# A gated mix of linear attention and a GLU in one kernel: the key sums with the values as stationary operand, 64-partition matmuls filled to 128, and another order of the stages

## The chip, the cores and the metric

One core of a Trainium2 chip runs the whole program. The time is device microseconds of one execution. Six streams of work matter in the profile: PE (matrix multiplication) and PEld (the loading of its stationary operand), DVE, ACT and POOL (elementwise engines), and SP, which here only issues DMAs. ACT and POOL issue DMAs too. Every engine works through its own list strictly in order, so one instruction that waits holds up all that stand behind it on that engine.

## The reference

The inputs are x (2048 tokens by 576), the attention weights, three GLU weights and a gate vector. Linear attention with 32 heads of 18 and a tanh-GELU GLU of width 4608 are mixed per token.

```python
def _A_ref(x, wqkv, wo):
    B, S, D = x.shape
    H = 32; Dh = D // H
    qkv = (x @ wqkv).reshape(B, S, 3, H, Dh).transpose(2, 0, 3, 1, 4)
    q, k, v = qkv[0], qkv[1], qkv[2]
    phi = lambda t: jnp.where(t > 0, t + 1, jnp.exp(t)) + 1e-6
    pq, pk = phi(q), phi(k)
    kv = jnp.einsum("bhsd,bhse->bhde", pk, v)
    z = jnp.einsum("bhsd->bhd", pk)
    num = jnp.einsum("bhqd,bhde->bhqe", pq, kv)
    den = jnp.einsum("bhqd,bhd->bhq", pq, z)[..., None] + 1e-6
    return (num / den).transpose(0, 2, 1, 3).reshape(B, S, D) @ wo

def _B_ref(x, w_gate, w_up, w_down):
    return (gelu(x @ w_gate) * (x @ w_up)) @ w_down

g = sigmoid((x * gate_w).sum(-1, keepdims=True))
return g * _A_ref(x) + (1 - g) * _B_ref(x)
```

## The kernel before

**Numbers.** Operands are split into a high part (written in fp32r) and a low part (the rest); a product is high x high + high x low + low x high.

**Key loop** (lines 187 to 238, up to 147 us). For each of 16 tiles of 128 tokens the kernel projects keys, values and the gate (42 matmuls), applies phi to the keys, and `kv_state` adds the tile's keys times values into `acc_a` and `acc_b`: for each of five groups of seven heads (the last has four), one matmul with the high keys and one with the low keys as stationary operand (126 columns, 72 in the last group), and the values as moving operand: two columns of ones, the high and the low values, 254 columns in all (146 in the last group). All four products come out, low by low too; the column of ones gives z.

**Stage order** (lines 440 to 735). The stages behind it are written out by hand as words in four lists; `run` calls them one after the other, and this sets the order of every engine. A word is a letter and one or two indices:

- `Qbg`, `abg`: the query projection of token block b (four blocks of 512 tokens) and column group g into one of three PSUM banks (14 matmuls of 512 columns, 10 for g = 4), and phi on ACT and DVE. `hbg` splits it on ACT and DVE; `dbg` adds it to the denominators (two matmuls, one for g = 4).
- `s`, `z`, `t`, `u`: copy out the state, write z to DRAM and read it back, mask and transpose the state on PE, split it. `n` makes the denominator's weights of z. `wg`, `ig`, `og`, `fg`: load wo's part, split it, multiply the state by it, store the result in DRAM; `lg`, `cg`: load that back and split it into KW.
- `rb`: the reciprocals of block b's denominators, in two halves. ACT copies one part of a half out of PSUM, DVE adds the other and inverts; SP stores 18 copies per head in DRAM (`rden_d`) and loads them back spread over the partitions (`rb`).
- `pbt`, `mbt`, `ebt`: scale the queries of token tile t (DVE, ACT, DVE), multiply by KW (28 matmuls of 288 columns into one of two pairs of banks; the last two use 64 partitions, since the last group has 64 rows), copy out on ACT with the gate and store by ACT's queue.
- `Xk`, `yk`, `Yk`: load a part of x, form four sums of token blocks on DVE, write their high parts on ACT and low parts on POOL into `xo`. The sums overwrite slots of `xo` that held blocks 2 and 3; `x` stores those in DRAM first (three DMAs). X1 and X2 are issued by POOL, into one buffer. `Wm`: load the first weights of the GLU. `Gk`, `gk`: the GLU's first products.

**The GLU** (from about 306 us) is a loop over 36 steps whose order is a table that stays as it is.

Of the kernel before, what the change touches and what calls it, by code (L numbers as in the profile page):

```python
# [21 lines left out]
NG = 5  # L22
# [5 lines left out]
CW = 126 + NG * 64 + 128  # L28
# [22 lines left out]
def tile_gated_mix(ctx, tc, xt, xs, wkv, wq, wo, wgu, wgt, wdn, cst, out):  # L51
# [8 lines left out]
    rden_d = {(b, h): dram.tile([H, DH, BS // 2], F32, name=f"rden_d{b}{h}") for b in range(NB) for h in range(2)}  # L60
# [130 lines left out]
    for v in vbuf:  # L191
        nc.vector.memset(f32(v).rearrange("p (g c) -> p g c", g=NG)[:, :, 0:2], 1.0)

    def kv_post(t, c, ps, part):
        if c == 0:
            pk[t] = (kp.tile([128, D], F32, name="e"), kp.tile([128, D], F32R, name="pkh"),
                     kp.tile([128, D], F32R, name="pkl"))
            vt[t] = vbuf[t % 2]
        r, ph, pl = pk[t]
        v3 = vt[t].rearrange("p (g c) -> p g c", g=NG)  # L200

        def k_part(lo, n):
# [24 lines left out]
    def kv_state(t):  # L227
        _, ph, pl = pk.pop(t)
        v = vt.pop(t)
        for g in range(NG):  # L230
            w = 2 + 2 * GR[g]
            mv = v[:, g * VW:g * VW + w]
            if g < 4:
                o = acc_a[:GR[g], g // 2, (g % 2) * VW:(g % 2) * VW + w]
            else:
                o = acc_b[:GR[g], 0, :w]
            for i, p in enumerate((ph, pl)):
                nc.tensor.matmul(o, p[:, GO[g]:GO[g] + GR[g]], mv,  # L238
                                 start=(t == 0 and i == 0 and g in (0, 2, 4)),
                                 stop=(t == NST - 1 and i == 1), skip_group_check=True)  # L240
# [160 lines left out]
    rs = [rp.tile([128, NG, BS], F32, name=f"r{i}") for i in range(3)]  # L401
    r_of = {2: rs[0], 3: rs[1], 0: rs[2], 1: rs[0]}
# [63 lines left out]
    wide = acc_a[:126, :, :2 * VW].rearrange("p a (b c) -> p a b c", b=2)  # L466
    last = acc_b[:72, 0]

    def sums_out():
        nc.vector.tensor_copy(zc[:126, :4].rearrange("p (a b) -> p a b", a=2), wide[:, :, :, 0])  # L470
        nc.vector.tensor_copy(zc[:72, 4:5], last[:, 0:1])

# [3 lines left out]
        nc.sync.dma_start(at(0, [[1, 126], [126, 4]]), zc[:126, :4])  # L476
        nc.sync.dma_start(at(504, [[1, 72], [1, 1]]), zc[:72, 4:5])
# [15 lines left out]

    turned = []

    def states_turn():
        tps = pair()
        turned[:] = [tps[:GR[g], g // 4, (g % 4) * 126:(g % 4) * 126 + GR[g]] for g in range(NG)]
        for g in range(NG):
            R = GR[g]  # L500
            nc.tensor.transpose(turned[g], kvm[:R, g, :R], ident[:R, :R])
# [27 lines left out]
    def head_out(g):  # L529
# [3 lines left out]
        kh, kl = kvt[:R, g, 0, :R], kvt[:R, g, 1, :R]  # L533
# [557 lines left out]
```

## Time and profile before

| | us |
|---|---|
| median of 3 runs (lowest, highest) | 1527.63 (1524.12, 1532.23) |
| the profiled execution | 1529.19 |
| its span, first to last instruction | 1527.4 |
| PE busy in the span | 1505.2 |
| key loop with its start, from the span's start to the first query | 146.8 |
| stage order, first query to the last token tile's output | 159.6 |

A row that groups instructions reads: line, engine, operation, output<-inputs, shapes, count, then busy time, mean ns of one, idle time before them and what ended it. A row of the chain of waits has a start, a length and what the time went to. PE's matmuls overlap, so the mean of one is longer than the distance of two starts; distances are taken from the chain.

### The profile page before, as it was taken

To read this page: it belongs to the slowest core of one execution; us is meant where nothing else is said; L and a number is where in the kernel's file an instruction comes from. 1 tells how busy PE (TensorE), PEld (TensorE's weight loads), DVE (VectorE), ACT (ScalarE), POOL (GpSimd) and SP (SyncE) were. 2 spreads that over 40 slices of the span, in tenths; PEclk is the share of its full clock that TensorE was granted. 3 is DMA by queue.
4 is the path that set the end of the run, shared out by engine and by line. 5 is a ranking of instruction groups with operands and counts; after the bars stand their busy time and mean duration, and the time that the engine had idled before them with its cause. 6 is when DMAs were issued, how large, how long until landed. Compare 5 with 4: busy or idle time off the path is not lost.

```text
span 1527.4 us, 21407 instructions
## 1 busy us (share of the span) xinstructions
PE 1505.2 (99%) x8179; PEld 1326.5 (87%) x8179; DVE 1106.8 (72%) x1693; ACT 578.8 (38%) x967; POOL 745.2 (49%) x710
## 2 busy tenths in 40 slices
PE   8999999999999999999999999999999999999998
PEld 8999778788888888888888888888888888888887
DVE  6444567578888888888887777777777777777776
ACT  6555655334334333343434323223222222232223
POOL 1474222167878788788776724323233223232323
PEclk9999999999999999999999999999999999999999
DMA  5676666655665667656556475433443344334441
GB/s 202 201 257 224 204 170 218 211 190 200 220 226 205 226 241 261 235 204 222 201 193 225 143 303 206 179 146 137 175 173 136 136 158 175 137 145 184 181 173 62
DMA packets 117884, 293.57 MB, mean 192 GB/s; under 512 B 6806, under 2 KB 88918, under 8 KB 107414
## 3 DMA queue, kind: packets, MB, share of 16 engines
q1 hardware_dynamic: 114258, 279.48, 52.1%
q10 hardware_dynamic: 3236, 10.63, 1.9%
q0 software_dynamic: 288, 2.10, 0.4%
q8 instruction: 64, 1.05, 0.3%
q14 instruction: 38, 0.31, 0.1%
HBM read 177.15 MB, written 115.03 MB: 191 GB/s over the span
## 4 chain that ended last, share of the span: by engine, by line
PE 92%; DMA 3%; POOL 2%; issue 2%; ACT 1%; DVE 1%; SPq 0%; POOLq 0%; DVEq 0%; ACTq 0%
PE bank L694 52%; PE pair L791 25%; PE bank L187 8%; PE pair L633 3%; PE bank L421 1%; PE pair L238 1%; DMA raw<-wo 1%; POOL xo L660 1%; DMA xo<-xop_d 1%; DMA xc<-xs 1%; POOL sums L781 0%; POOL kw L557 0%; PE pair L187 0%; PE pair L993 0%; DMA raw<-wkv 0%
## 5 line engine op out<-in xcount | busy, mean ns | idle before, releaser
L713 DVE TENSOR_TENSOR sums<-pair,sums 128x576 f32<-128x576 f32 x474 | 354.6, 754 | 160.9 <-PE pair L791 149.0
L694 PE MATMUL bank<-xo,wg 128*128 128x512 f32 x1764 | 442.0, 393 | 5.1 <-POOL xo L660 2.4
L694 PE MATMUL bank<-xo,wu 128*128 128x512 f32 x1764 | 430.4, 393 | 0.8 <-DVE p L713 0.8
L694 PEld LDWEIGHTS bank<-xo,wu 128*128 128x128 f32 x1764 | 323.8, 188 | 64.3 <-DVE p L713 1.2
L694 PEld LDWEIGHTS bank<-xo,wg 128*128 128x128 f32 x1764 | 322.5, 188 | 65.6 <-POOL xo L660 3.6
L791 PEld LDWEIGHTS pair<-wd,h 128*128 128x128 f32 x1680 | 248.2, 189 | 17.3
L791 PE MATMUL pair<-wd,h 128*128 128x288 f32 x1680 | 259.2, 296 | 0.0
L791 PEld LDWEIGHTS pair<-wd,hx 128*128 128x128 f32 x1260 | 179.1, 189 | 9.3
L791 PE MATMUL pair<-wd,hx 128*128 128x288 f32 x1260 | 184.4, 295 | 0.0
L707 ACT ACTIVATE p<-bank 128x512 f32<-128x512 f32 x72 | 43.0, 597 | 354.5 <-PE bank L694 348.3
L857 POOL TENSOR_TENSOR wd<-draw,wd 128x432 fp32r<-128x432 f32 x68 | 75.1, 1123 | 191.8 <-ACT wd L707 191.8
L833 POOL TENSOR_TENSOR h<-e,h 128x512 fp32r<-128x512 f32 x70 | 96.4, 1377 | 140.6 <-ACT h L707 140.6
L833 POOL TENSOR_TENSOR hx<-e,hx 128x512 fp32r<-128x512 f32 x70 | 96.6, 1401 | 112.7 <-ACT hx L707 112.7
L707 ACT ACTIVATE h<-e 128x512 fp32r<-128x512 f32 x107 | 67.3, 629 | 211.9 <-DVE e L713 211.9
L849 POOL TENSOR_TENSOR work<-work 128x256 f32<-128x256 f32 x136 | 113.4, 844 | 6.0 <-DMA work<-wgu 0.6
L187 PE MATMUL bank<-kvw,xo 128*128 128x378 f32 (+5 forms) x560 | 106.9, 345 | 5.8 <-ACT kvw L81 5.7
L187 PEld LDWEIGHTS bank<-kvw,xo 128*128 128x128 f32 (+1 forms) x560 | 97.3, 192 | 10.3 <-ACT kvw L81 6.2
L713 DVE TENSOR_TENSOR u<-bank,p 128x512 f32<-128x512 f32 x72 | 49.6, 689 | 47.1 <-PE bank L694 32.3
L707 ACT ACTIVATE hx<-e 128x512 fp32r<-128x512 f32 x105 | 63.9, 626 | 35.2 <-DVE e L713 35.2
L713 DVE TENSOR_TENSOR e<-bank,e 128x512 f32<-128x512 f32 x106 | 72.5, 684 | 1.2
L707 ACT ACTIVATE wd<-draw 128x864 fp32r<-128x864 f32 (+1 forms) x35 | 32.7, 934 | 99.3 <-PE pair L791 99.3
L633 PE MATMUL pair<-kw,p 128*128 128x288 f32 x448 | 66.0, 301 | 0.4 <-POOL kw L557 0.3
(173 smaller groups left out, 1829.1 us busy)
## 6 DMA issues: line engine op xcount, KB each, us to landing
wg<-wp_d SPq DMA_DIRECT2D x17, 2240.0 KB
wu<-wp_d SPq DMA_DIRECT2D x17, 2240.0 KB
wp_d<-wg SPq DMA_DIRECT2D x16, 2240.0 KB
wp_d<-wu SPq DMA_DIRECT2D x16, 2240.0 KB
draw<-wdn SPq DMA_DIRECT2D x35, 576.0 KB
work<-wgu SPq DMA_DIRECT2D x34, 512.0 KB
xo<-xop_d SPq DMA_DIRECT2D x7, 1280.0 KB
wt_d<-tail_op SPq DMA_DIRECT2D x15, 448.0 KB
```

What stands on the lines that cost most here:

```text
L187: nc.tensor.matmul(out_t[:, :n], xa, kvw[i][:rows, r, lo:lo + n], start=(k == 0), stop=(k == 13))
L238: nc.tensor.matmul(o, p[:, GO[g]:GO[g] + GR[g]], mv, start=(t == 0 and i == 0 and g in (0, 2, 4)), stop=(t == NST - 1 and i == 1), skip_gr ...
L421: nc.tensor.matmul(ps, qw[i][:rows, c:c + 128], xa, start=(k == 0), stop=(k == 13))
L633: nc.tensor.matmul(y[:, i, :288], pa, w[:, i * 288:(i + 1) * 288], start=(n == 0), stop=(n == 13))
L660: nc.gpsimd.tensor_tensor(xo[rows, S2 + k, lo], raw[rows, k], f32(xo[rows, S2 + k, kt]), OP.subtract)
L694: nc.tensor.matmul(ps, w_, x_, start=start and i == 0, stop=i == 6, skip_group_check=not start)
L707: nc.scalar.activation(o, i, AF.Copy)
L713: nc.vector.tensor_tensor(o, a, b, op)
L791: nc.tensor.matmul(pr[q][:, j, :288], h[:, hl, c], wd[:, b, wl], start=start and i == 0, stop=i == 2, skip_group_check=not start)
L833: op(name + "l", lambda n, e, a=a, f=src_of: e.tensor_tensor(hb[a][:, 1], f(), f32(hb[a][:, 0]), sub))
L849: op(f"{name}T{i + 1}", lambda n, e, o=o, a=a, b=b: e.tensor_tensor(o, a, b, sub))
L857: op(f"dl{x}{j}", lambda n, e, i=i, src=src, c=c: e.tensor_tensor(wd[:, i, 1, c], src[:, :, c], f32(wd[:, i, 0, c]), sub))
```

## The change

**The state** is formed with the values as stationary operand. For each group one matmul has 128 stationary columns (126 high values and two columns of ones) and moves the high and the low keys (252 columns), and a second has the low values and moves the high keys alone (126). The low by low product falls away, and the state comes out transposed, with z as row 126, so the step `t` and its identity matrix go; z is stored in DRAM as one row. In the last group the two are 144 and 72 columns wide.

PE at one token tile of the key loop (vt are the values, pk the keys, the pair holds the sums):

```order
-L238 MATMUL pair<-vt_224,pkh 126x254
-L238 MATMUL pair<-vt_224,pkl 126x254
-L238 MATMUL pair<-vt_224,pkh 72x146
-L238 MATMUL pair<-vt_224,pkl 72x146
+L234 MATMUL pair<-pk,vt_224 128x252
+L236 MATMUL pair<-pk,vt_224 126x126
+L234 MATMUL pair<-pk,vt_224 128x144
+L236 MATMUL pair<-pk,vt_224 72x72
```

The first two rows of each sort stand there four times, once for each full group; ten matmuls stay ten.

**64 partitions to 128.** The second half of KW's low part for the last group is set to zero once, and the last two matmuls of a token tile read all 128 partitions.

**The reciprocals** are stored 9 times instead of 18 and loaded with each row read twice: six loads for a half instead of two, of the same bytes.

```diff
     def kv_state(t):
-        _, ph, pl = pk.pop(t)
+        p = pk.pop(t)[1]
         v = vt.pop(t)
         for g in range(NG):
-            w = 2 + 2 * GR[g]
-            mv = v[:, g * VW:g * VW + w]
...
-            for i, p in enumerate((ph, pl)):
-                nc.tensor.matmul(o, p[:, GO[g]:GO[g] + GR[g]], mv,
-                                 start=(t == 0 and i == 0 and g in (0, 2, 4)),
-                                 stop=(t == NST - 1 and i == 1), skip_group_check=True)
+            R, k = GR[g], slice(GO[g], GO[g] + GR[g])
+            o = acc_a[:, g // 2, (g % 2) * 252:(g % 2 + 1) * 252] if g < 4 else acc_b[:, 0, :2 * R]
+            nc.tensor.matmul(o, v[:, g * VW:g * VW + 128], p[:, :, k], start=(t == 0 and g in (0, 2, 4)),
+                             stop=False, skip_group_check=True)
+            nc.tensor.matmul(o[:R, :R], v[:, g * VW + 128:g * VW + 128 + R], p[:, 0, k], start=False,
+                             stop=(t == NST - 1), skip_group_check=True)
...
+    nc.vector.memset(f32(KW)[64:, 1, 4], 0.0)
...
+        nc.sync.dma_start(at(0, [[D, 1], [1, D]]), kvm[126:127])
...
-    def states_turn():
...
     def states_split():
-        for g in range(NG):
-            R = GR[g]
-            split(kvt[:R, g, 0, :R], kvt[:R, g, 1, :R], turned[g])
+        f = kvm[:126, :504].rearrange("p (g c) -> p g c", g=4)
+        nc.vector.tensor_tensor(f, f, bass.AP(tensor=mask.tensor, offset=mask.offset,
+                                              ap=[[mask.ap[0][0], 126], [0, 4], [1, 126]]), OP.mult)
+        nc.vector.tensor_tensor(kvm[:72, 504:], kvm[:72, 504:], mask[:72, :72], OP.mult)
+        split(kvt[:126, 0], kvt[:126, 1], kvm[:126])
...
-            nc.sync.dma_start(rb[:, :4], bass.AP(
-                tensor=src.tensor, offset=src.offset, ap=[[HB, 128], [128 * HB, 4], [1, HB]]))
-            nc.sync.dma_start(rb[:, 4], bass.AP(
-                tensor=src.tensor, offset=src.offset + 512 * HB, ap=[[0, 2], [HB, 64], [1, HB]]))
+            for g in range(NG):
+                n = min(64, H * DH // 2 - 64 * g)
+                for k in range(64 // n):
+                    nc.sync.dma_start(rb[64 * k:64 * k + 64, g] if n < 64 else rb[:, g], bass.AP(
+                        tensor=src.tensor, offset=src.offset + 64 * g * HB, ap=[[HB, n], [0, 2], [1, HB]]))
...
-        ops += [(p[:, 0, 4], KW[:, 0, 4]), (p[:64, 0, 4], KW[:64, 1, 4])]
+        ops += [(p[:, 0, 4], KW[:, 0, 4]), (p[:, 0, 4], KW[:, 1, 4])]
```

**The order.** All four lists are new. The lines that the prediction speaks of, first the piece around the third block's queries, then the one around the second token sums:

```diff
-r2 h30 c2 Q03 c4 h32 a03 Q33 c3 d30 a33 Q04 h31 d31 d32 h33 a04 p21 l1 h34 X0 Q02 a02 p20 d33 Q01 d34 r3 Q00
+h22 d22 c1 Q32 l2 a30 h23 l3 d23 h24 X0 h30 d24 Q31 c4 a33 c2 r2 d30 a32 c0 a31 c3 h32 h31 Q01 a01 Q34 d31 h33
+a34 Q00 p20 d32 Q04 h34 a00 d33 a04 p21 h00 m20 x Q02 y0 h01 d34 m21 Q03 r3 d00 h04 d01 a02 a03 h02 Q10 h03
...
-c0 c1 a00 Q14 a01 m21 h00 h01 m20 p23 d00 e20 e21 Q10 y0 p22 m23 m22 d01 Y0 a10 Q12 X1 h04 a14 p31 h02 d02 e22
-Q11 e23 p30 h03 y1 d03 d04 r0 a12 m30 e30 a11 m31 h10 Q13
+d02 Q11 e20 d03 p23 m23 Y0 p22 a10 d04 e21 p31 m22 h10 e23 p30 X1 y1 r0 a11 m31 e31 Q14 e22 m30 Y1 a14 p33 h11
+Q12 a12 d10 Q13 d11 e30 m33 p32 h12 d12 a13
```

SP from the head's weights on, before (wo is loaded by `w`, `xop_d<-xo` is `x`, `kwr` is `l`, `rden_d` and `rb` are `r`):

```order
L519 DMA raw<-wo 128x576 x2
L476 DMA z_d<-zc 126x4x1
L477 DMA z_d<-zc 72x1
L478 DMA zq<-z_d 128x4x1
L479 DMA zq<-z_d 128x1x1
L519 DMA raw<-wo 128x576
L581 DMA xop_d<-xo 128x2560 x3
L519 DMA raw<-wo 128x576 x2
L549 DMA kwr<-kw_d 128x576 x3
L552 DMA kwr<-kw_d 64x576 x2
L607 DMA rden_d_70<-rb 576x1x256
```

SP at the same place now, from the last four weight loads:

```order
L499 DMA raw<-wo 128x576 x4
L529 DMA kwr<-kw_d 128x576
L532 DMA kwr<-kw_d 64x576 x2
L529 DMA kwr<-kw_d 128x576 x3
L627 DMA xc<-xs 128x2048
L587 DMA rden_d_70<-rb 288x1x256
L587 DMA rden_d_71<-rb 288x1x256
L593 DMA rb<-rden_d_70 128x1x256 x4
L593 DMA rb<-rden_d_70 64x1x256 x2
L593 DMA rb<-rden_d_71 128x1x256 x4
L593 DMA rb<-rden_d_71 64x1x256 x2
L561 DMA xop_d<-xo 128x2560 x3
```

The three stores of `x` stood ahead of two weight loads, and now stand behind all weight loads and the whole round trip of block 2's reciprocals.

ACT from block 0's reciprocals to the second token sums' split, before (`rb<-den` is r0, r is the queries' tile, `ga` with its DMA is `e`, p is `p`, `xo<-xc` is Y1):

```order
L604 ACTIVATE rb<-den 32x256 x2
L435 ACTIVATE r_1677<-bank 128x512
L436 ACTIVATE r_1677<-r_1677 128x512
L638 ACTIVATE ga<-pair,gate 128x576
L640 DMA ga_d_89<-ga 128x576
L435 ACTIVATE r_1677<-bank 128x512
L436 ACTIVATE r_1677<-r_1677 128x512
L565 ACTIVATE hl<-r_1677 128x512 x2
L638 ACTIVATE ga<-pair,gate 128x576
L640 DMA ga_d_90<-ga 128x576
L621 ACTIVATE p<-r_1678 128x640
L657 ACTIVATE xo<-xc 128x4x512
```

ACT at the same place now:

```order
L584 ACTIVATE rb<-den 32x256 x2
L433 ACTIVATE r_1663<-bank 128x512
L434 ACTIVATE r_1663<-r_1663 128x512
L619 ACTIVATE ga<-pair,gate 128x576
L621 DMA ga_d_90<-ga 128x576
L619 ACTIVATE ga<-pair,gate 128x576
L621 DMA ga_d_87<-ga 128x576
L638 ACTIVATE xo<-xc 128x4x512
```

Behind r0 there now stand a11, two stored token tiles (e31 and e22) and then Y1; before, the tile of block 2 had been stored ahead of r0.

More of the change, by code (lines that the diff above doesn't have):

```diff
@@ L59, in tile_gated_mix @@
     gate = keep.tile([128, 2, NST], F32, name="gate")
-    rden_d = {(b, h): dram.tile([H, DH, BS // 2], F32, name=f"rden_d{b}{h}") for b in range(NB) for h in range(2)}
+    rden_d = {(b, h): dram.tile([H, DH // 2, BS // 2], F32, name=f"rden_d{b}{h}") for b in range(NB) for h in range(2)}
     z_d = dram.tile([D, 1], F32, name="z_d")
@@ L191, in tile_gated_mix @@
     for v in vbuf:
-        nc.vector.memset(f32(v).rearrange("p (g c) -> p g c", g=NG)[:, :, 0:2], 1.0)
+        v = f32(v).rearrange("p (g c) -> p g c", g=NG)
+        nc.vector.memset(v[:, :, 126:128], 1.0)
+        nc.vector.memset(v[:, 4, 72:126], 0.0)
     def kv_post(t, c, ps, part):
         if c == 0:
-            pk[t] = (kp.tile([128, D], F32, name="e"), kp.tile([128, D], F32R, name="pkh"),
-                     kp.tile([128, D], F32R, name="pkl"))
+            pk[t] = (kp.tile([128, D], F32, name="e"), kp.tile([128, 2, D], F32R, name="pk"))
             vt[t] = vbuf[t % 2]
-        r, ph, pl = pk[t]
+        r, (ph, pl) = pk[t][0], (pk[t][1][:, i] for i in range(2))
         v3 = vt[t].rearrange("p (g c) -> p g c", g=NG)
@@ L453, in tile_gated_mix @@
     cs = tp.tile([128, CW], F32, name="cs")
-    kvm = tp.tile([128, NG, 126], F32, name="kvm")
-    kvt = tp.tile([128, NG, 2, 126], F32R, name="kvt")
-    zc = tp.tile([128, NG], F32, name="zc")
+    kvm = tp.tile([128, D], F32, name="kvm")
+    kvt = tp.tile([128, 2, D], F32R, name="kvt")
     zq = tp.tile([128, NG], F32, name="zq")
     nc.sync.dma_start(cs, cst)
-    mask, sel, ident = cs[:, :126], cs[:, 126:126 + NG * 64], cs[:, 126 + NG * 64:]
+    mask, sel = cs[:, :126], cs[:, 126:]
     def gates():
@@ L464, in gates, with states_out @@
         nc.vector.tensor_scalar(gate[:, 1], gate[:, 0], -1.0, 1.0, op0=OP.mult, op1=OP.add)
-    wide = acc_a[:126, :, :2 * VW].rearrange("p a (b c) -> p a b c", b=2)
-    last = acc_b[:72, 0]
+    def states_out():
+        wide = acc_a[:, :, :504].rearrange("p a (b h c) -> p a b h c", b=2, h=2)
+        four = (lambda v: v[:, :504].rearrange("p (a b c) -> p a b c", a=2, b=2))
+        last = acc_b[:, 0, :144]
+        low = tp.tile([128, D], F32, name="low")
+        nc.scalar.activation(four(low), wide[:, :, :, 1], AF.Copy)
+        nc.scalar.activation(low[:, 504:], last[:, 72:], AF.Copy)
+        nc.vector.tensor_tensor(four(kvm), wide[:, :, :, 0], four(low), OP.add)
+        nc.vector.tensor_tensor(kvm[:, 504:], last[:, :72], low[:, 504:], OP.add)
@@ L532, in head_out @@
         y = y_of[g] = pair()
-        kh, kl = kvt[:R, g, 0, :R], kvt[:R, g, 1, :R]
+        kh, kl = (kvt[:R, i, GO[g]:GO[g] + R] for i in range(2))
         for k, (ka, wl) in enumerate(((kh, 0), (kh, 1), (kl, 0))):
@@ L581, in keep_x @@
             nc.sync.dma_start(xop_d[:, a], f32(x_slot(b, i)))
-    STEPS.update(v=gates, z=sums_out, s=states_out, t=states_turn, u=states_split, n=den_weights, w=wo_load, i=wo_split,
+    STEPS.update(v=gates, z=sums_out, s=states_out, u=states_split, n=den_weights, w=wo_load, i=wo_split,
                  o=head_out, f=head_store, l=kw_load, c=kw_split, h=halves_of, d=den, x=keep_x)
     run("""
-w2 Q21 w0 v Q22 s z a21 t i2 i0 Q24 h21 a22 u a24 Q34 a34 w3 o2 Q20 x Q32 Q31 n i3 f2 o3 a20 a32 h20 o0 f3 w4
-i4 f0 w1 i1 Q23 a23 d20 o4 d21 f4 h22 o1 l2 l3 h23 f1 l0 Q30 l4 h24 a31 a30 d22 d23 d24
+s Q24 a24 w1 i1 Q20 u z w2 i2 Q21 Q23 a21 o1 a20 h21 o2 w4 i4 f1 w0 i0 Q22 n f2 o4 a23 f4 h20 w3 i3 o0 Q30 f0
+l1 l4 d20 v a22 o3 l0 f3 d21 Q33
     """)
@@ L675, in tile_gated_mix @@
     run("""
-h11 e31 p32 d10 d11 Y1 p33 m32 h12 d12 a13 e32 p01 m33 W0 h13 h14 e33 p00 X2 y2 d13 m01 d14 r1 m00 Y2
+W0 m32 p01 h13 d13 X2 h14 e33 e32 m01 p00 d14 y2 m00 r1 Y2
     """)
@@ L733, in tile_gated_mix @@
     run("""
-G1 G6 G7 g1 p03 G2 e01 m03 p02 g6 e00 g7 e03 m02 p10 m10 e02 p11 m11 W1 p13 e10 p12 e11 g2 m13 e13 m12 e12
+G1 G6 g1 G2 p02 e01 p03 e00 G7 g6 m02 e02 m03 g7 p10 m10 e03 p11 m11 W1 p13 e10 p12 e11 m13 g2 e13 m12 e12
     """)
```

38 lines of the change are left out of this document (6 added, 32 removed).

## The prediction

> **What bounds the kernel now.** I read the page first: its span, its engines, its chain.
>
> ```profile
> span 1527.4 us, 21407 instructions
> PE 1505.2 (99%) x8179; PEld 1326.5 (87%) x8179; DVE 1106.8 (72%) x1693; ACT 578.8 (38%) x967; POOL 745.2 (49%) x710
> ```
>
> PE is the bound; 1% of the span is its idle time. So an edit is worth PE time: instructions taken from PE, instructions made shorter, or waits ended. The diff touches two stretches: the state matmuls of the key loop (24 to 147 us) and the hand-written stage order behind it, from the first query (146.8 us) to the last token tile of the attention output (306.4 us). The second by the windows view:
>
> ```profile
> 146.77:306.41 159.64, 151.74 (x812) 127.02 (x811) 94.61 (x146) 84.23 (x135) 33.65 (x24) 0.98 0.62 194
> 160.00:180.00 20.00, 18.13 (x82) 15.01 (x81) 8.50 (x18) 12.97 (x22) 4.29 (x3) 0.91 0.79 303
> 270.00:282.00 12.00, 8.53 (x29) 5.69 (x28) 6.98 (x9) 4.04 (x5) 6.08 (x4) 0.86 0.59 144
> ```
>
> Columns: window, length, busy PE, PEld, DVE, ACT, POOL, clock, DMA. DVE and ACT are little over half busy in the 159.6 us, so they can only hurt by order. The granted clock falls twice, each time where PE idled: (1 - 0.91) x 20 = 1.8 us and (1 - 0.86) x 12 = 1.7 us lost, 3.5 together. PE's waits there:
>
> ```profile
> PE bank L694 <- POOL xo L660: 2.4, 1, 2.4
> PE den L576 <- DVE hl L567: 2.0, 2, 1.7
> PE bank L694 <- ACT p L707: 1.1, 1, 1.1
> PE pair L536 <- POOL wos L526: 1.0, 1, 1.0
> PE pair L536 <- ACT wos L525: 0.9, 1, 0.9
> PE pair L633 <- POOL kw L557: 0.3, 1, 0.3
> ```
>
> They sum to 7.7 us. What PE's work itself needs, by the chain of waits (start, length, what):
>
> ```profile
> 180.10 3.24 PE bank L421 x14
> 238.58 0.70 PE den L576 x3
> 281.96 24.45 PE pair L633 x168
> 326.46 1.60 PE bank L694 x7
> 336.89 1.60 PE pair L791 x12
> ```
>
> A 512-column matmul takes 0.23 us (3.24/14, 0.70/3, 1.60/7), a 288-column one 0.133 (1.60/12). The stage has 264 query and 36 denominator matmuls (300 x 0.231 = 69.3), 28 of the first GLU products (6.4), 30 + 448 of 288 columns (63.7): 139.4 us. Its 159.6 hold 20.2 more: 7.7 waits, 3.5 clock, and three terms below.
>
> **Part 1: 64-row matmuls filled to 128.** Of a token tile's 28 output matmuls two read 64 partitions (32 of 448).
>
> ```profile
> L633 PE MATMUL pair<-kw,p 128*128 128x288 f32 x416 | 59.2, 298 | 0.4 <-POOL kw L557 0.3
> L633 PE MATMUL pair<-kw,p 64*128 64x288 f32 x32 | 8.4, 343 | 0.0
> ```
>
> The 168 in the chain row take 0.1455 each against 0.1333 for the same shape without such neighbours: 0.0122 x 448 = **5.5 us**. By the two form rows alone it would be (8.4/32 - 59.2/416) x 32 = 3.9; busy time does not show what the neighbours lose, so 5.5. If the zero half of the weight tile cost something, it would be its one memset on DVE, which has free time there.
>
> **Part 2: no transposes.** Five leave PE. Two of their weight loads start
>
> ```profile
> 153.22 0.14 PEld L501 LDWEIGHTS pair<-cs,kvm 126*126 126x126 f32 x1
> 153.33 0.14 PEld L501 LDWEIGHTS pair<-cs,kvm 126*126 126x126 f32 x1
> ```
>
> 0.11 us apart: 5 x 0.11 = **0.5 us**. The five copies, five subtractions and five masks on ACT and DVE become one, one and two; PE did not wait for them (no kvt row above), so 0.
>
> **Part 3: the state matmuls.** Ten per token tile stay ten; the columns streamed fall from 8 x 254 + 2 x 146 = 2324 to 4 x (252 + 126) + 144 + 72 = 1728.
>
> ```profile
> 44.00 1.08 PE pair L238 x10
> 139.06 0.23 PE L238 MATMUL pair<-vt,pkh 128*72 128x146 f32 x1
> 139.13 0.23 PE L238 MATMUL pair<-vt,pkl 128*72 128x146 f32 x1
> ```
>
> The starts of the last two are 0.07 us apart (146 columns); the ten take 1.08, so one of 254 takes (1.08 - 2 x 0.07) / 8 = 0.12: some 0.47 ns a column, and 596 columns x 0.47 x 16 tiles = 4.5 us if columns set the pace. But each matmul has its own weights, and the 126-column transposes above, loading 126 columns too, came no closer than 0.11, not 0.06. With 0.11 for each short matmul the ten take 4 x (0.12 + 0.11) + 0.07 + 0.11 = 1.10: nothing won. From below: ten at 0.12, 1.6 us lost. I take **0.6**, near the load row.
>
> The Trainium skill ("TensorE: Matmul & The Clock Gate", Back-to-back issue gap) speaks for more: a sustained stream of weight load and matmul at 128 columns takes about 81 ns each. By that the ten take 0.95 and 2.1 us are won; the rows here show 0.11, from transposes, and decide until the new matmuls are seen.
>
> **Part 4: the order.** Steps are named as in the code (Q query, a activation, o and f head output, p m e scaled, mixed, stored token tile, X y Y token sums, r reciprocals).
>
> *What goes.* The two wos waits: SP issued three 1280 KB stores (x) ahead of a weight load, and that load landed 13.7 us late (first row).
>
> ```profile
> 160.59 13.69 DMA raw<-wo
> 184.65 0.38 ACT L604 ACTIVATE rb<-den 32x256 f32<-32x256 f32 x1
> 195.63 0.53 SPq L612 DMA_DIRECT2D rb<-rden_d  x1
> 200.79 0.83 DVE L620 SCALAR_TENSOR_TENSOR r<-r,rb 128x640 f32<-128x640 f32 x1 [2.80 <-DMA rb<-rden_d]
> 257.44 10.27 DMA xc<-xs
> ```
>
> Now all five weight loads and block 2's reciprocals go first (SP's rows in the section on the change). By the next two rows SP needs 11.5 us from r2's start to its last load; x follows, when PE has done Q31, Q01, Q34 and Q00 (3 x 3.2 + 2.3 = 12 us), and lands some 14 us on, near m21's end. Its first reader, Y0, comes 10 us later, and block 3's reciprocals are stored as x ends. The hl wait came from DVE standing 2.8 us at p20, 16.1 us after r2's start. Now p20 comes behind a34: Q31, Q01, Q34 and two denominators (9.2) and a34's five operations (3.2), so 12.4 us after r2's start. It needs 2.8 us (0.8, a copy, two subtractions), and m20 comes 16.2 us after r2 (0.5, Q00, 0.5, Q04, 0.5 more). With the round trip as before m20 would wait 16.1 + 2.8 - 16.2 = 2.7 us; with half the bytes stored it should be near 0, which I take. The POOL wait (Y2) came from X2, which took 10.3 us (last row) with y2 waiting for it. X2 now starts as soon as POOL has done Y1, about 10 us ahead of y2. The clock loss goes with the waits. **7.7 + 3.5 = 11.2 us**.
>
> *What comes.* On DVE, y1 now stands right behind p30, and X1 is issued only when POOL has done Y0; r0 is queued behind y1, and ACT behind r0. The prices:
>
> ```profile
> 251.17 5.98 POOL xo L660 x4
> DMA to landing us min/median/max: 5.5/7.9/10.3
> 239.14 0.69 DVE L653 TENSOR_TENSOR xc<-xc 128x512 f32<-128x512 f32 x1
> 239.75 0.40 DVE L605 TENSOR_TENSOR rb<-rb,den 32x256 f32<-32x256 f32 x1
> 240.19 0.38 ACT L604 ACTIVATE rb<-den 32x256 f32<-32x256 f32 x1 [0.49 <-DVE rb L605]
> 240.59 0.60 ACT L435 ACTIVATE r<-bank 128x512 f32<-128x512 f32 x1
> 241.22 0.63 ACT L436 ACTIVATE r<-r 128x512 f32<-128x512 f32 x1
> 243.23 0.74 ACT L638 ACTIVATE ga<-pair,gate 128x576 f32<-128x576 f32 x1 [1.38 <-PE pair L633]
> 244.00 0.33 ACTq L640 DMA_DIRECT2D ga_d<-ga  x1
> 249.16 1.90 ACT L657 ACTIVATE xo<-xc 128x2048 fp32r<-128x2048 f32 x1
> L567 DVE SCALAR_TENSOR_TENSOR hl<-r,hl 128x512 fp32r<-128x512 f32 x16 | 13.0, 821 | 2.6 <-ACT hl L565 2.3
> ```
>
> ACT's second reciprocal copy waits for DVE's first sum (the 0.49), and on ACT a11, e31 and e22 are queued behind it; m30 needs e22 for its pair of banks. The chain from Y0's copy: 1.9 (ACT) + 6.0 (POOL) + 5.5 (X1, the lowest of two landings) + 2.8 (y1) + 0.4 + 0.4 + 1.2 (a11) + 0.7 + 0.3 (e31) + 0.7 (e22) + 0.4 of hand-overs = 20.3 us. PE meanwhile, from m23: m23, d04, m22, m31, Q14 = 3 x 3.73 + 0.23 + 2.3 = 13.8. Both start at Q03's end: Y0's copy 6.2 us later (a03's 1.2 on ACT; its 0.7, two hl of 0.8 and p23's 0.8 on DVE; p23's copy, 640 elements at ACT's 0.60 for 512, 0.75; 1.1 of hand-overs and of DVE's queue), m23 8.3 us later (Q10 and Q11, 6.4; eight denominator matmuls, 1.9: d00 to d03). 6.2 + 20.3 - 8.3 - 13.8 = **4.4 us of new wait** at m30, and the clock falls after so long an idle as in the two old places: **1.7**. With X1 at 10.3 it would be 9.2; if Y0 ran before p23, under 3.
>
> *The rest.* 48 loads of rb stand for 16, the same bytes; SP's issue of one is 0.4 to 1.4 us, so up to some us per block, inside the slack of r2, r3 and r0 by the sums above; r1 has some 1 us. W0, issued on ACT behind a13, has about 2 us. I charge 0 and leave this to the range. Neither the key loop's other engines nor the GLU loop after 306 us change.
>
> **Sum:** 5.5 + 0.5 + 0.6 + 11.2 - 4.4 - 1.7 = 11.7 us. The profiled execution took 1529.19 (span 1527.4), 1.6 above the median of 1527.63; 11.7 off gives 1517.5 for it and 1515.9 for the median: **1516**.
>
> **Rivals.** *No new wait* (Y0 comes earlier than my sum, or e22 slips in): 6.1 better, 1510. For: ACT and DVE are half idle. Against: POOL and X1 alone are 11.5 us of the chain. *State set by columns*: 3.9 better, 1512; for it the 0.07 row, against it the 0.11. *The waits move instead of going*: the 11.2 is given back in other places by such chains (p20, d11, p10 have about 1 us), 6.6 is left: 1521. *Part 1 is not the shape* but the end of each group: 5.5 less, 1521.5; against it the two form rows. *Slower:* SP's 12 loads per block. This row bounds their issue:
>
> ```profile
> L612 SPq DMA_DIRECT2D rb<-rden_d x8: 526/717/1412, 192.7 to 280.8; - x8
> ```
>
> Eight more at 1.4 each are 11 us per block on a queue in order; less the slack of 2 to 4, three blocks (2, 0, 1) would wait 7 us each, 21 in all, and lose the clock three times (5): 26 against 17.8 won without the forecast's wait, 1536. It decides from about 7 us more per block; the 0.4 us of most of SP's issues speaks against.
>
> **How the numbers follow.** Forecast 0.60 (1516); no new wait 0.12; state by columns 0.10; waits move 0.10; part 1 wrong 0.04; slower 0.04. About 0.5% (7.6 us) is what a measurement can tell from no change: faster is under 1520.0, slower over 1535.3. X1's other end (4.8 us) puts some of the forecast over 1520, so faster 0.78, same 0.17, slower 0.05. Range: down to no new wait with the columns' gain, 1506, up to the 1521 cases and X1's end, 1524.
>
> **What would show it.** Right: L633 matmuls 0.133 apart; no L501; state groups near 1.05; no wos or hl wait on PE; DVE at the second token sums waiting for xc; one PE wait of about 4 us for ACT ga, with a clock dip. Wrong: state groups near 0.8; PE waiting for p after rb; a wait at the first GLU products; the stage from first query to last token tile longer than 150 us.

## The result and the profile after

| | before | after |
|---|---|---|
| median, runs side by side (us) | 1529.01 (1524.12 to 1532.23, 7 runs) | 1518.82 (1518.29 to 1520.86, 7 runs) |
| profiled execution, its span (us) | 1529.19, 1527.4 | 1518.65, 1516.5 |
| ratio of the times, 95% interval | | 0.9938 (0.9922 to 0.9953) |

The change makes the kernel 0.6% faster, about 10 us; 11.7 were forecast. The page of the changed kernel:

```profile
span 1516.5 us, 21429 instructions
PE 1495.5 (99%) x8174; PEld 1325.2 (87%) x8174; DVE 1106.4 (73%) x1687; ACT 577.0 (38%) x963; POOL 746.6 (49%) x710
```

The same stretches by the windows view (window, length, busy PE, PEld, DVE, ACT, POOL, clock, DMA):

```profile
146.31:296.10 149.79, 142.94 (x808) 126.38 (x807) 95.03 (x140) 83.21 (x132) 34.66 (x24) 0.98 0.59 190
160.00:180.00 20.00, 20.00 (x97) 16.73 (x96) 12.53 (x21) 15.42 (x29) 9.02 (x6) 1.00 0.65 208
225.00:240.00 15.00, 11.75 (x65) 10.40 (x64) 9.48 (x13) 6.81 (x10) 3.33 (x3) 0.89 0.51 163
262.00:274.00 12.00, 8.40 (x33) 6.57 (x32) 6.07 (x9) 3.56 (x6) 5.78 (x4) 0.86 0.46 131
```

The first query starts 0.46 us earlier (146.77 before), and the stage order takes 149.8 us for 159.6. The clock's fall at 160 to 180 us is gone (experiment 1 shows what that is worth). But it still falls twice: (1 - 0.89) x 15 = 1.65 us and (1 - 0.86) x 12 = 1.7 us. PE's waits in that stretch have become two:

```profile
PE bank L676 <- ACT p L689: 3.6, 1, 3.6
PE pair L614 <- ACT ga L619: 3.2, 1, 3.2
```

Waits of 7.7 us in sum have gone, and two of 6.8 us in sum have come. In the chain of waits the token tiles behind the first GLU products stand in one piece:

```profile
146.31 2.40 PE bank L422 x10
273.71 22.39 PE pair L614 x168
```

22.39 / 168 = 0.1333 us for one output matmul, where it was 0.1455.

**The wait that was forecast.** The timeline of the changed kernel around m30 (start, length, what, in brackets the idle time ahead and what ended it):

```profile
221.23 0.70 POOL L627 DMA_DIRECT2D xc<-xs  x1 [0.31 <-POOL xo L641]
...
227.61 0.69 DVE L631 TENSOR_TENSOR xc<-xc 128x512 f32<-128x512 f32 x1 [1.90 <-DMA xc<-xs]
...
230.84 0.38 ACT L584 ACTIVATE rb<-den 32x256 f32<-32x256 f32 x1 [5.76 <-DVE rb L585]
231.24 0.60 ACT L433 ACTIVATE r<-bank 128x512 f32<-128x512 f32 x1
...
232.40 0.72 ACT L619 ACTIVATE ga<-pair,gate 128x576 f32<-128x576 f32 x1
...
233.18 2.12 PE L614 MATMUL pair<-kw,p 128*128 128x288 f32 x11 [3.25 <-ACT ga L619]
...
233.53 0.74 ACT L619 ACTIVATE ga<-pair,gate 128x576 f32<-128x576 f32 x1 [0.40 <-ACT ga L619]
```

It is the chain of the prediction link by link: X1 is issued, y1 waits for it, r0's second copy on ACT waits 5.76 us for DVE, a11 follows, then a stored token tile, and PE starts 0.06 us behind that. One link was read wrongly: PE starts behind the first of the two stored tiles (e31, done at 233.12), while e22 begins only at 233.53. So m30 takes the pair of banks that e31 releases.

**The wait that was to go, and stayed.** The same view around the second GLU product, G2:

```profile
243.22 0.57 POOL L627 DMA_DIRECT2D xc<-xs  x1 [0.31 <-POOL xo L641]
...
253.97 0.74 ACT L619 ACTIVATE ga<-pair,gate 128x576 f32<-128x576 f32 x1 [1.75 <-PE pair L614]
...
255.12 0.74 ACT L602 ACTIVATE p<-r 128x640 fp32r<-128x640 f32 x1 [0.40 <-ACT ga L619]
...
256.93 0.69 DVE L631 TENSOR_TENSOR xc<-xc 128x512 f32<-128x512 f32 x1
...
260.44 1.90 ACT L638 ACTIVATE xo<-xc 128x2048 fp32r<-128x2048 f32 x1
...
262.43 5.78 POOL L641 TENSOR_TENSOR xo<-xc,xo 32x512 fp32r<-32x512 f32 x4 [18.64 <-ACT xo L638]
...
268.24 0.60 ACT L689 ACTIVATE p<-bank 128x512 f32<-128x512 f32 x1 [5.90 <-POOL xo L641]
...
268.89 4.82 PE L676 MATMUL bank<-xo,wg 128*128 128x512 f32 x14 [3.60 <-ACT p L689]
```

X2 takes 7.3 us from its issue at 243.22, so it is there at 250.5, and nobody waits for it any more. y2 still starts only at 256.93, because it stands on DVE behind p00, p00's copy on ACT behind e32, and e32 waits for PE. From there y2, Y2's copy and its four operations on POOL take 11.3 us. The last step is a buffer: `p1`, which ACT writes at L689, lies in memory that the token sums held, so the copy waits for POOL's last reading of them, and G2 waits for the copy. The kernel before has the same link, and PE's 1.1 us for ACT p there come from it:

```profile
279.42 0.60 ACT L707 ACTIVATE p<-bank 128x512 f32<-128x512 f32 x1 [6.21 <-POOL xo L660]
```

### The profile page after: what moved, and what is told of

It reads as the page before. It is cut to its first block, busy times and chain, and to the rows that moved or that the text cites. A ratio compares the mean times of both kernels' runs of the same rounds, so it can differ in the third digit from the quotient of the medians.

```text
span 1516.5 us, 21429 instructions
## 1 busy us (share of the span) xinstructions
PE 1495.5 (99%) x8174; PEld 1325.2 (87%) x8174; DVE 1106.4 (73%) x1687; ACT 577.0 (38%) x963; POOL 746.6 (49%) x710
## 3 DMA queue, kind: packets, MB, share of 16 engines
q8 instruction: 64, 1.05, 0.3%
## 4 chain that ended last, share of the span: by engine, by line
PE 93%; issue 1%; DMA 1%; DVE 1%; POOL 1%; ACT 1%; POOLq 0%; SPq 0%; DVEq 0%; ACTq 0%
PE bank L676 53%; PE pair L773 26%; PE bank L187 7%; PE bank L419 2%; PE pair L614 2%; PE pair L234 1%; DMA xo<-xop_d 1%; POOL xo L641 1%; POOL sums L763 0%; DMA xc<-xs 0%; PE pair L187 0%; PE pair L975 0%; PE bank L422 0%; PE pair L236 0%; DMA raw<-wkv 0%
## 5 line engine op out<-in xcount | busy, mean ns | idle before, releaser
L695 DVE TENSOR_TENSOR sums<-pair,sums 128x576 f32<-128x576 f32 x474 | 354.5, 754 | 161.7 <-PE pair L773 149.8
L689 ACT ACTIVATE p<-bank 128x512 f32<-128x512 f32 x72 | 43.0, 597 | 355.1 <-PE bank L676 349.2
L689 ACT ACTIVATE h<-e 128x512 fp32r<-128x512 f32 x107 | 67.3, 629 | 210.7 <-DVE e L695 210.7
L689 ACT ACTIVATE hx<-e 128x512 fp32r<-128x512 f32 x105 | 63.9, 626 | 35.1 <-DVE e L695 35.1
L689 ACT ACTIVATE wd<-draw 128x864 fp32r<-128x864 f32 (+1 forms) x35 | 32.7, 934 | 99.3 <-PE pair L773 99.3
L614 PE MATMUL pair<-kw,p 128*128 128x288 f32 x448 | 62.8, 300 | 3.2 <-ACT ga L619 3.2
```

Of the source, the lines that this page charges most:

```text
L614: nc.tensor.matmul(y[:, i, :288], pa, w[:, i * 288:(i + 1) * 288], start=(n == 0), stop=(n == 13))
L689: nc.scalar.activation(o, i, AF.Copy)
L695: nc.vector.tensor_tensor(o, a, b, op)
```

## The experiments

The theory after this reading: the order removed 7.7 us of waits and brought 6.8 back, so the gain is the PE work saved by the other parts. The rival: the parts are not worth their PE time by themselves, and something else in the change made room. All ratios below are to the kernel before, run on the same chip in the same hours (medians 1526.7 to 1526.9). The changed kernel was not run again beside them; its 1518.82 us stood against 1529.01. So what experiments 5 to 7 gain on it in us is about 1.4 us less by the ratios, and what experiment 11 loses is about 1 us more.

### 1. The fill alone

```diff
+    nc.vector.memset(f32(KW)[64:, 1, 4], 0.0)
-        ops += [(p[:, 0, 4], KW[:, 0, 4]), (p[:64, 0, 4], KW[:64, 1, 4])]
+        ops += [(p[:, 0, 4], KW[:, 0, 4]), (p[:, 0, 4], KW[:, 1, 4])]
```

> The kernel before with one edit: the second half of the low weight of the last group is zero and the last two matmuls of a token tile read 128 partitions. Theory (the 64-row shape costs its neighbours too): the 168 output matmuls behind the first GLU products go from 24.45 us to about 22.4 us, as in the changed kernel, and the time falls by 5.5 to 6.3 us, ratio 0.9959 to 0.9964. Rival 1 (the end of each group costs it, whatever the shape): nothing, ratio 1.000, 24.4 us. Rival 2 (only the mean durations of the two shapes differ): 3.9 us, ratio 0.9974.

Measured: 1527.19 us, ratio 1.0003 (0.9994 to 1.0013): nothing. Yet the matmuls are shorter, as in the changed kernel (chain of waits), while PE's waits have grown (waits of PE, then of DVE, then X1 and X2 from issue to landing):

```profile
280.29 22.38 PE pair L634 x168
```

```profile
PE bank L695 <- POOL xo L661: 4.7, 2, 3.9
PE den L577 <- DVE hl L568: 2.7, 3, 1.4
PE bank L695 <- DMA wg<-wp_d: 2.5, 1, 2.5
PE bank L695 <- ACT p L708: 1.1, 1, 1.1
```

```profile
DVE xc L651 <- DMA xc<-xs: 7.2, 1, 7.2
DVE r L621 <- DMA rb<-rden_d: 2.9, 2, 2.5
```

```profile
DMA to landing us min/median/max: 5.3/9.3/13.4
```

In place of 2.4 us for POOL there are 4.7, and 2.5 for W0 (the GLU's weights) that did not exist before. X2 needs 13.4 us for 10.3. So the shape does cost what was forecast, as rival 1 denies, but the time won ahead of the first GLU products is waited away there: with the old order and the old loads that place is set by transfers. The 2.1 us won behind them (22.38 for 24.45) go on the clock, which is 0.86 at 260 to 285 us for 0.93 in the kernel before. (The profiled execution, 1525.61 us, is the fastest of eleven; the median says more.)

The head of the stage is the same here as in the kernel before, with the three stores of x ahead of two weight loads, and yet the wait for wos is 0.2 us for 1.9, and the clock does not fall at 160 to 180 us, where it was 0.91:

```profile
PE pair L537 <- POOL wos L527: 0.2, 1, 0.2
160.00:180.00 20.00, 19.84 (x96) 16.55 (x95) 10.03 (x21) 15.62 (x27) 4.32 (x3) 1.00 0.79 299
```

The other six profiles with the old order (experiments 2, 3, 8 to 10 and 12) show the same: wos 0 to 0.6 us, clock 1.00. As far as these profiles tell, the 1.9 us of wait and the 1.8 us of clock behind it belong to the one profiled execution of the kernel before, and not to its order.

### 2. The state and the missing transposes alone

The edit is the first two parts of the diff in the section on the change with the old lists, 64-row matmuls and loads.

> The kernel before with the new state matmuls and without the transposes, the old order (its step t dropped), the old loads of the reciprocals and the old 64-row matmuls. Theory: ten state matmuls take 1.02 us for 1.08 as in the changed kernel, about half of that is given back by the projections behind them, and the five transposes take 0.5 us with them: 1.0 to 1.6 us less, ratio 0.9990 to 0.9993, and the sums of PE's waits stay near 7.7 us. Rival (the new copies and masks of the state come later than the old ones on the way to the first head output): the wait for wos or hl grows and the time does not fall, ratio 1.000 or above.

Measured: 1525.39 us, ratio 0.9994 (0.9985 to 1.0003). The ten state matmuls take 1.02 us, counted from start to start; the sum cannot be told from no change, and it is not more than was expected.

### 3. All parts but the order

```diff
-s Q24 a24 w1 i1 Q20 u z w2 i2 Q21 Q23 a21 o1 a20 h21 o2 w4 i4 f1 w0 i0 Q22 n f2 o4 a23 f4 h20 w3 i3 o0 Q30 f0
+w2 Q21 w0 v Q22 s z a21 i2 i0 Q24 h21 a22 u a24 Q34 a34 w3 o2 Q20 x Q32 Q31 n i3 f2 o3 a20 a32 h20 o0 f3 w4
...
```

> The changed kernel with the four lists of the kernel before (step t dropped): all parts but the order. Theory (the order took two waits away and brought one of its own, so it is worth only about 3 us): some 3 us above the changed kernel, ratio 0.9953 to 0.9960, with PE's waits for wos, hl and POOL xo back, about 7 us in sum, and both clock dips. Rival 1 (the order is worth the 11 us that its waits cost): ratio 1.000 or above. Rival 2 (the twelve loads of the reciprocals hurt where the order does not make room): waits for p or hl above 3 us more than before, ratio 0.998 or above.

Measured: 1517.28 us, ratio 0.9941 (0.9925 to 0.9956), against 0.9938 of the changed kernel: **the new order adds nothing** that can be measured, less than the 3 us of the theory. PE's waits in the stage are 5.0 us in sum, for about 7 expected: the wait for wos does not come back, nor does the clock's fall behind it, and the others are those of before:

```profile
PE bank L675 <- POOL xo L641: 2.6, 2, 2.2
...
PE den L556 <- DVE hl L547: 1.3, 2, 1.0
PE bank L675 <- ACT p L688: 1.1, 1, 1.1
```

Experiments 1 and 2 give 0.9997 if multiplied; this kernel has besides them only the new stores and loads of the reciprocals, whose loads the prediction charged at 0. Experiments 8 to 11 take that up.

### 4. What sets the pace of the state matmuls

```diff
-            nc.tensor.matmul(o, v[:, g * VW:g * VW + 128], p[:, :, k], start=(t == 0 and g in (0, 2, 4)),
+            o_, p_ = (o, p[:, :, k]) if t == 0 else (o[:, :R], p[:, 0, k])
+            nc.tensor.matmul(o_, v[:, g * VW:g * VW + 128], p_, start=(t == 0 and g in (0, 2, 4)),
```

> The changed kernel, in which, from the second token tile on, the wide state matmul moves the high keys alone (126 columns for 252, 72 for 144 in the last group), so high values by low keys are left out; the count of matmuls and of weight loads stays. Theory (the weight loads of 126 and 128 columns set the pace, about 0.11 us each): the ten of a token tile still take 0.95 to 1.02 us. Rival (the columns set it, 0.42 to 0.47 ns each): 4 x (126 + 126) + 72 + 72 columns, about 0.6 us.

Measured: 1519.48 us in one execution; ten matmuls take 0.98 us for 1.02. Some starts of the changed kernel, and then of this one, in the timeline:

```profile
144.34 0.33 PE L234 MATMUL pair<-pk,vt 128*128 128x252 f32 x1
144.51 0.22 PE L236 MATMUL pair<-pk,vt 128*126 128x126 f32 x1
144.56 0.34 PE L234 MATMUL pair<-pk,vt 128*128 128x252 f32 x1
```

```profile
69.50 0.27 PE L235 MATMUL pair<-pk,vt 128*128 128x126 f32 x1
69.61 0.27 PE L237 MATMUL pair<-pk,vt 128*126 128x126 f32 x1
69.72 0.28 PE L235 MATMUL pair<-pk,vt 128*128 128x126 f32 x1
```

A wide and a narrow one together take 0.22 us (144.34 to 144.56); with the wide one halved they still take 0.22, now 0.11 each. So the columns that move do not set it. Nor does a fixed time of any matmul: the two with 72 stationary columns in the prediction's rows start 0.07 us apart. What is left is the load of 126 or 128 stationary columns.

The Trainium skill ("TensorE: Matmul & The Clock Gate", Back-to-back issue gap) gives about 81 ns for a matmul of 128 columns in a sustained stream of weight loads and matmuls. By that, as an estimate, the halved pair would take 0.16 us; here it takes 0.22.

### 5. The reciprocals of block 0 behind the stored tiles

```diff
-h10 e23 p30 X1 y1 r0 a11 m31 e31 Q14 e22 m30 Y1 a14
+h10 e23 p30 X1 a11 m31 e31 Q14 e22 m30 y1 r0 Y1 a14
```

> The changed kernel with y1 and r0 behind e22 and ahead of Y1. Theory (m30's wait of 3.2 us is the chain X1, y1, r0, a11, e31, e22, as forecast): the wait goes and the clock's fall at 233 to 238 us with it, 5 us less than the changed kernel, about 1513.8 us, ratio 0.990. Rival 1 (e22 stands there for another reason, or the wait moves to the next token tile or to p01 for the later reciprocals): 1517 to 1519 us, ratio 0.993. Rival 2 (a slower m30 had covered the second wait: it grows by what is won here): nothing won, the wait for ACT p about 8 us.

Measured: 1513.70 us, ratio 0.9914 (0.9901 to 0.9928). The wait for ACT ga is gone, that for ACT p is still 3.6 us, and the kernel is 5.1 us faster than the changed one (1518.82), 3.7 by the ratios. The forecast chain is the cause of the wait.

### 6. The third token sums earlier

```diff
-W0 m32 p01 h13 d13 X2 h14 e33 e32 m01 p00 d14 y2 m00 r1 Y2
+W0 m32 p01 X2 y2 h13 h14 e33 e32 Y2 m01 d13 p00 d14 m00 r1
```

> The changed kernel with y2 and Y2 ahead (y2 behind p01, Y2 behind e32, r1 last; the denominators d13 and d14 stand together behind m01). Theory (G2's wait of 3.6 us for ACT p is the last link of y2, Y2's copy and Y2's four operations on POOL, of which y2 starts 6 us after X2 has landed): the wait goes, with the clock's fall at 269 to 272 us, 5 us less than the changed kernel, about 1513.8 us, ratio 0.990. Rival 1 (X2's landing bounds it): 1517 to 1519 us. Rival 2 (p00, now behind y2, is late for m00): a wait for p of 1 us or more in its place, 1515 us or more.

Measured: 1513.80 us, ratio 0.9915 (0.9901 to 0.9928); the wait for ACT p is gone and that for ACT ga 3.4 us. That is 5.0 us, 3.5 by the ratios, for the place of y2 and Y2: X2 did not bound it.

### 7. Both moves: a version that beats both kernels

The edit is that of 5 and 6 together.

> Both moves in one kernel. Theory (the two waits are independent): 10 us less than the changed kernel, about 1508.5 us, ratio 0.9867, no wait of PE over 0.5 us between the first query and the last token tile, that stretch near 139.5 us, no fall of the clock in it. Rival (PE comes to the first GLU products 5 us earlier, and X2 does not): the second wait is back by 2 to 5 us, 1511 to 1514 us.

Measured: 1509.62 us (1509.33 to 1510.38), ratio **0.9887** (0.9874 to 0.9901), 9.2 us faster than the changed kernel, 7.8 by the ratios. The stage by the windows view, and all of PE's waits in it:

```profile
146.30:286.61 140.31, 139.67 (x804) 123.36 (x803) 95.10 (x140) 82.66 (x130) 34.43 (x24) 1.00 0.63 203
```

```profile
PE pair L614 <- ACT p L602: 0.2, 1, 0.2
PE den L556 <- DVE hl L547: 0.2, 1, 0.2
```

140.3 us, clock 1.00: the 139.4 us of plain matmul work that the prediction counted, and hardly more. The two waits are independent of each other.

### 8. to 10. The stores and loads of the reciprocals

Alone in the kernel before, and with the fill:

```diff
-            nc.sync.dma_start(rb[:, :4], bass.AP(
-                tensor=src.tensor, offset=src.offset, ap=[[HB, 128], [128 * HB, 4], [1, HB]]))
-            nc.sync.dma_start(rb[:, 4], bass.AP(
-                tensor=src.tensor, offset=src.offset + 512 * HB, ap=[[0, 2], [HB, 64], [1, HB]]))
+            for g in range(NG):
+                n = min(64, H * DH // 2 - 64 * g)
+                for k in range(64 // n):
...
```

> The kernel before with the new stores and loads of the reciprocals alone (stored 9 times, six loads for a half). The fill alone moved nothing and all parts but the order moved 0.59%, so these loads carry the difference, alone or with the fill. Theory (a set of transfers decides when the first GLU products start: block 0's reciprocals, X2 and W0 one after the other; PE time won ahead of it is waited away, and the shorter round trip moves the set itself forward): DVE's wait for rb (2.8 us) and PE's for hl (2.0) go, 3 to 5 us less, ratio 0.997 to 0.998. Rival 1 (the loads are worth all of it): 8 us, ratio 0.9948. Rival 2 (the loads alone do nothing, since PE is then the bound): 0.999 or above.

> The kernel before with the fill and the new stores and loads, the old order and the old state. Theory (the fill is paid out in full once the transfers are early enough): all parts but the order gave 0.9941, less about 1 us of the state: ratio 0.9945 to 0.9950. Rival (the state and the missing transposes are what made room): 0.998 or above.

And with the fill, the old stores and the old wide load, but the narrow load of the last group in two:

```diff
-            nc.sync.dma_start(rb[:, 4], bass.AP(
-                tensor=src.tensor, offset=src.offset + 512 * HB, ap=[[0, 2], [HB, 64], [1, HB]]))
+            for k in range(2):
+                nc.sync.dma_start(rb[64 * k:64 * k + 64, 4], bass.AP(
+                    tensor=src.tensor, offset=src.offset + 512 * HB, ap=[[HB, 64], [1, HB]]))
```

> The kernel before with the fill, the old stores (18 copies) and the old wide load, but the load of the last group's 64 rows, which reads them twice in one transfer with an outermost dimension of 2 and took 6.8 to 9.7 us for 128 KB, is written as two transfers of 64 rows. Theory (this one slow load is the late end of each round trip): its landing comes 2 to 3 us after the wide load's issue-to-landing is over for the others, and half or more of the 8 us is won, ratio 0.9955 to 0.998. Rival (the bytes of the stores, twice as many, are what is slow): 0.999 to 1.000.

| old order, old state | old loads | narrow load split | new stores and loads |
|---|---|---|---|
| 64-row matmuls | 1 | not run | 0.9974 (0.9964 to 0.9984) |
| filled to 128 | 1.0003 (0.9994 to 1.0013) | 0.9958 (0.9945 to 0.9970) | 0.9949 (0.9935 to 0.9962) |

The loads are worth 4 us by themselves and 8 with the fill; the fill is worth nothing without them and about 4 us with them. Most of it hangs on the one narrow load: two lines that split it, with the same bytes, make 1.0003 into 0.9958. X1 and X2 from issue to landing and the waits of PE and of DVE in that kernel, to be read against the rows of experiment 1:

```profile
DMA to landing us min/median/max: 5.7/7.6/9.4
```

```profile
PE bank L696 <- POOL xo L662: 3.1, 2, 2.7
```

```profile
DVE xc L652 <- DMA xc<-xs: 3.2, 1, 3.2
```

X2 takes 9.4 us for 13.4, DVE waits 3.2 for it instead of 7.2 and not at all for rb, and PE's 2.5 us for W0 are gone. The narrow load itself is late: counted in the traces from its issue to its last completion, the eight of experiment 1 take 7.6 to 11.2 us, and the sixteen halves of this kernel 2.0 to 6.3. Each of the eight has two late completions where the wide load beside it has sixteen. In the kernel before, the first one lands 8.0 us after its issue at 192.71, at 200.70, and p20 on DVE starts at 200.79; the wide load beside it had landed at 197.99. So DVE's 2.8 us for rb, from which the hl wait came, are the narrow load's.

That it also delays X2 is not shown as clearly: with it X2 takes 9.6, 10.3 and 13.4 us (experiment 2, the kernel before, experiment 1), without it 9.4 to 9.5 in four profiles (experiments 3 and 8 to 10).

### 11. The new order with the old stores and loads

> The changed kernel with the old stores and loads of the reciprocals. Theory (the new order leaves little room at m20, as the prediction worked out: 2.7 us of wait with the round trip as before, and X2 is delayed by the longer transfers): 3 to 6 us above the changed kernel, ratio 0.9958 to 0.998. Rival 1 (the order leaves room enough): 0.9938. Rival 2 (the waits that the order brings double): 1.000 or above.

Measured: 1523.28 us, ratio 0.9975 (0.9966 to 0.9983), 4.5 us above the changed kernel. The waits that the order brings are longer, m20's wait for p has come (0.8 us, where the prediction worked out 2.7 for the old round trip), and DVE waits for rb:

```profile
PE pair L613 <- ACT ga L618: 5.0, 2, 4.6
PE bank L675 <- ACT p L688: 3.9, 1, 3.9
...
PE pair L613 <- ACT p L601: 0.8, 1, 0.8
```

```profile
DVE r L600 <- DMA rb<-rden_d: 3.8, 2, 2.7
```

With the old loads the order does help: 0.9975 here against the 0.9997 that experiments 1 and 2 give if multiplied (these two in one kernel with the old order were not run). By these times order and loads answer the same delay, and with the loads there is nothing left for this order to win.

### 12. Where the 64-row matmuls lose their time

```diff
-        ops += [(p[:, 0, 4], KW[:, 0, 4]), (p[:64, 0, 4], KW[:64, 1, 4])]
+        ops += [(p[:64, 0, 4], KW[:64, 0, 4]), (p[:64, 0, 4], KW[:64, 1, 4])]
```

> The kernel before with four matmuls of 64 rows in a row at the end of a token tile for two: of the last group the low part of the queries by the high weights is left out, which makes its two matmuls 64 rows too. Theory A (each matmul of 64 rows and its neighbour pay: about 0.1 us at every one of the steps into, between and out of them): six such steps a token tile for four, the six token tiles behind the first GLU products near 25.6 us for 24.45. Theory B (only a change of the shape pays, at its two edges): 24.45 us as before, the two steps between 64-row matmuls 0.13 us.

Measured in one execution (1526.38 us): the distances of starts, medians counted in the trace for 288 columns, in us:

```
step                          two of 64 rows   four of 64 rows
128 rows to 128, elsewhere    0.131            0.132
128 to 64                     0.226            0.229
first 64 to second            0.236            0.235
second to third, to fourth    -                0.131, 0.132
64 to 128                     0.222            0.226
first 128 to the next         0.238            0.238
```

Theory B with one addition: each change of shape costs two steps of 0.1 us, itself and the one behind it, and matmuls of one shape then run at full pace. Four steps a token tile whether two or four of its matmuls have 64 rows. The sum that the expectation named does not decide by itself: the six token tiles took 25.28 us, near theory A's 25.6, but their first 1.7 us ran at half clock, which costs about 0.8; without it they are at theory B's 24.45.

```profile
278.82 25.28 PE pair L633 x168
278.82:280.53 1.71, 1.71 (x8) 1.71 (x8) 0.99 (x3) 1.25 (x2) 0.00 (x0) 0.50 0.86 265
```

The Trainium skill ("TensorEngine Tiling (Array Packing)", Key Properties) says that a change of the tiling mode drains TensorE. The steps of 0.22 to 0.24 us at each change, for 0.131, agree.

## Why the prediction was right, and where it was not

The time lay in the range and 2.9 us above the forecast; against the kernel before as it ran beside it the gain was 10 us for 11.7. That the number is so near is in part luck: a term of chance (wos) and a term put at 0 (the loads) went opposite ways. The terms, by the rows above:

| term (us) | forecast | in the profiles |
|---|---|---|
| 64-row matmuls | 5.5 | (24.45 - 22.39) x 448 / 168 = 5.5 |
| transposes | 0.5 | L501 is gone; not seen apart, 0.5 put in the sum |
| state | 0.6 | first query 0.46 earlier |
| waits and clock gone | 11.2 | wos, hl, kw 4.2, clock 1.8; at the GLU 5.2 came back as 3.6 + 1.7: 5.9 |
| new wait and its clock | -6.1 | -(3.2 + 1.65) = -4.85 |
| sum | 11.7 | 7.5, of 10.9 by the spans |

- **What failed: "The clock loss goes with the waits. 7.7 + 3.5 = 11.2".** Of the place at the first GLU products only the first link was worked out, X2's landing, and that came true (7.3 us, there 6.4 us ahead of y2). The rest of the chain, e32, p00, y2, Y2, POOL, was never set against PE's work as it was done for m30. It gave 3.6 us and the fall of the clock; experiment 6 gets 5.0 back. The 1.1 us for ACT p, the last link of the same chain, stood in the 7.7 without a reason why they should go. So the rival "the waits move instead of going" was true of one of the two places.
- **What failed in the same term: "The two wos waits".** The prediction put them down to the order, from one profile. Seven other profiles with the old order have 0 to 0.6 us of them and no fall of the clock there (experiment 1). So of the 11.2 us some 3.7 (1.9 and 1.8) were chance of the profiled execution: they are gone without the new order too, and the sums from the two profiles, 7.5 and 10.9 us, give the change that much too much.
- **What failed: "I charge 0" for the 48 loads.** The prediction weighed only what their issue could cost. Their issue took 0.60 us in the median of 48, no PE wait came from it, and the slower rival fell. What it did not weigh is that they end a delay: 4 us alone, 8 with the fill (experiments 8 and 9). It did count on half the bytes stored for p20 to come in time, but it is the narrow load that was late (experiment 10 keeps the old stores). Their gain stands in the sum under other names, as the wait for hl and as the 64-row term.
- **What failed in the reasoning: "an edit is worth PE time".** It holds of the changed kernel, but not of each part. The fill's 5.5 us were real in the trace and worth nothing in the time until the transfers behind the first GLU products were early enough. The rival that the fill brings nothing was right on the time of the part alone, for a reason that it did not name.
- **Right:** m30's wait, its cause and size. 4.4 us were forecast and 3.2 came: m30 waits for e31 and not for e22, which takes 1.1 us off the chain, X1 took 6.3 us for 5.5 (both by the timeline), and 0.9 is left open on PE's side, whose 13.8 us of work add up to 13.7. Experiment 5 gets 5.1 us back by moving its cause.
- **Right: the state goes at the pace of weight loads.** Ten in 1.02 us for 1.05 forecast, and experiment 4 shows the pace. About half of 16 x 0.06 us arrives at the first query: counted in the traces from the first state matmul to the first query, six profiles with the old state take 117.9 to 118.1 us and seven with the new one 117.4 to 117.6. The 0.46 alone would not show it, since the first state matmul starts anywhere from 27.5 to 28.8 us in them. (By its own figures, ten at 0.12 would have lost 1.9 us, not 1.6; the 0.6 does not hang on it.)
- **Errors that cancelled.** The rows account for 7.5 us and the spans for 10.9. Counted from start to start, PE's gaps in the stage are 10.0 us before and 7.5 after, where the waits view has 7.7 and 6.8: a wait costs PE about 0.2 us more than its idle time, and some gaps are too short for the view. Likewise the steps behind the 64-row matmuls into 512 columns are not in the 5.5 (6.3 counted by starts). Together these are 2.4 of the 3.4 us. In the kernel before alone they are 2.3 and 0.8, which is what the prediction's count of the stage left open: of its 20.2 us over plain matmul work, the waits, the clock and the two terms that lie in the stage, 5.5 and 0.5, are 17.2. 0.6 more lie behind the stage (1527.4 - 306.41 = 1221.0 before, 1516.5 - 296.10 = 1220.4 now), where the code is the same and other profiles scatter as much; the rest was not traced further.

## What to carry to other kernels

Ahead of a place that waits for transfers, PE time saved is worth nothing until the transfers come earlier: find the next such place before summing up matmul savings, and try each part alone, since here two parts were worth 0 and 4 us apart and 8 together. Where a wait is said to go, work out the whole chain behind its first link, on every engine and down to the buffer that is written last, against PE's work in the same time; the same kind of sum that found the one wait here was not made for the other. Look for a wait in a second profile before counting on its end: the two for wos, 1.9 us in one profile, were 0 to 0.6 in seven others. A transfer that is slow for its bytes is to be rewritten before the order is searched anew: with the fill, splitting one load in two lines gave 0.45% of the time, where four new lists of the order gave 0.22% with the old loads (experiment 11 against 0.9997).

## What the runs showed of the hardware that was not expected

- A load of 128 KB whose outermost dimension repeats 64 rows twice lands late: 7.6 to 11.2 us after its issue, against 2.0 to 6.3 when it is written as two loads of 64 rows, and the kernel then took 0.45% less time (experiments 1 and 10).
- A change between matmuls of 64 and of 128 rows costs two steps of 0.1 us each time, however many of one shape follow; a run of 64-row matmuls goes on at 0.131 us (experiment 12).
- A chain of waits can differ between executions of one kernel: 21 runs of the kernel before lie between 1523.3 and 1529.7 us, four runs of the version without these waits between 1509.3 and 1510.4. That the waits are the cause is not shown.
